# When GpSimd starts, where a decay power is made, one weight difference half a pair later, one split on ScalarE

## The chip, the cores and the metric

The kernel runs on one core of a Trainium2 chip. The metric is the device time of one execution in microseconds (us). The core has five engines with a queue of instructions each: TensorE (PE) for matrix products, VectorE (DVE), ScalarE (ACT), GpSimd (POOL), and SyncE (SP), whose queue issues nearly all DMAs here. An engine works through its queue in order, so an instruction that waits holds up all that stand behind it.

## The reference

Two blocks are chained. The first is a linear attention with decay: for each batch element and head, a 48 x 48 state is multiplied by the decay w and receives the product of k and v at each of 768 steps. The second is a feed-forward block with the activation SoLU, h times softmax(h), followed by a layer norm and an output product.

```python
# r, k, v: (B 4, H 8, S 768, D 48) float32; w, u: (8, 48)
for t in range(S):
    kt, vt, rt = (k[:, :, t], v[:, :, t], r[:, :, t])
    cur = np.einsum('bhd,bhe->bhde', u[None] * kt, vt)
    y[:, :, t] = np.einsum('bhd,bhde->bhe', rt, state + cur)
    state = w[None, :, :, None] * state + np.einsum('bhd,bhe->bhde', kt, vt)
x = y.transpose(0, 2, 1, 3).reshape(B * S, H * D)   # 3072 x 384
h = x @ w_in                                        # 384 -> 1024, weights float64
sm = softmax(h)
solu = h * sm
ln = (solu - mean(solu)) / sqrt(var(solu) + 1e-06) * g_ln
out = ln @ w_out                                    # 1024 -> 384
```

## The kernel before

The sequence is cut into 24 chunks of 128 tokens (6 stretches of time for each of 4 batch elements; chunk `i` and chunk `i + 4` belong to the same batch element). All of a chunk's 8 heads are done together. Chunks are counted from 0. The order of all instructions is written out by hand: each engine's queue is the order of the calls in the program.

**Decay.** The decays w are loaded to `wq` (L494, by SP), transposed on TensorE (`wd_ps`, L636) and raised to powers by VectorE: `pw[:, 0, j]` is w to the power 2^j, and the table `tab` (L655) holds `back`, the powers from w^127 down to w^0, and `fore`, their inverses. Seven products build it, each twice as long as the one before; the last two have 256 and 512 elements in a row. `turn_table` (L663) transposes a table on TensorE and copies it with ScalarE to `kdec` or `rdec`.

**Attention.** For each chunk `decay_k` (L719) multiplies k by `kdec` on GpSimd and makes `kp`; `decay_r` does it with r and makes `rp`; `weigh` multiplies k, u and r on GpSimd (`rku`), and `sum_own` (L738) adds it up on VectorE to `own`, the weight of a token for itself. r and k are transposed. For chunks up to 8 TensorE does this (`turn_r`, `turn_k`), from chunk 9 on a transposing DMA does: `halve_k` (L1034, ScalarE) and `halve_r` (L1040) split the float32 words into 16-bit halves, `turn` issues the DMA from SP, and `join_rk` (L1052, VectorE) puts the words together again. `halve_r` runs on VectorE for chunks below `ON_ACT` and on ScalarE for the others. Then come the scores, their selection by a mask (`take_scores`), the state (`middle`, `update`) and y, which ScalarE copies to `xT`. From chunk 4 on `update` multiplies the new state by w^128 on GpSimd, which it reads from `wide` (L942).

**Feed-forward.** `ffn_in` makes 1024 hidden values in a PSUM tile of which there is one only (`h_ps`); ScalarE takes the exponentials (L957), VectorE multiplies (L964) and so frees `h_ps`. ScalarE then sums the squares. `halve_ln` and `join_ln` (L1017 through `join`) transpose a chunk's 1024 values through the DMA, to `lnT`, and `ffn_out` multiplies by `w_out_sb`. For chunks 4 and up two chunks are multiplied together with seven block products instead of eight, which need differences of blocks of the output weights. `weight_sums` (L1074) makes these on VectorE; the fourth is read in `both_c` (L1152).

**Weights.** They arrive as 64-bit words in 14 pieces of `raw`. `convert_a` (ScalarE), `convert_b` (VectorE) and `convert_c` (GpSimd, an add of integers) make float32 words of them.

**Phases.** The start (L1192 to L1267) does chunks 0 to 4 and converts six pieces. A loop over chunks 2 to 6 follows, one chunk a round. Then come chunks 7 and 8 (L1343 to L1384), and from L1386 a loop over pairs of chunks, of which the first round handles 9 and 10. In that loop `ffn_in`, `ffn_out` and the attention of three different pairs are interleaved. In its first round (`second_pair`) chunk 12's split is called right before `join_ln` of chunk 3.

The call of the differences stands ahead of the pair loop; `first` is chunk 11 in the first round:

```python
    join_ln(l + 2)
    weight_sums((1, 2, 4))
    sum_own(i + 5)
```

Of the kernel before, what the change touches and what calls it, by code (L numbers as in the profile page):

```python
# [9 lines left out]
F32 = mybir.dt.float32  # L10
U32 = mybir.dt.uint32
ACT = mybir.ActivationFunctionType
ALU = mybir.AluOpType
# [386 lines left out]
def direct_path(  # L400
# [29 lines left out]
    nc = tc.nc  # L430
    B, H, S, D = r.shape
    T = 128
    P = U = 64
# [5 lines left out]
    KF = dff // 128  # L439
    NX = 512  # L440
    LA, LO, FIRST, WHOLE, CHECKED = 2, 5, 9, 4, 15
    SEVEN, EARLY, ON_ACT = 4, 12, 13
    ROOM = {18: 4, 19: 5, 20: 3, 21: 2, 22: 1, 23: 0}
    LOW, HIGH = 0.75, 1.25

# [3 lines left out]
    const = ctx.enter_context(tc.tile_pool(name="const", bufs=1))  # L449
# [35 lines left out]
    wq = const.tile([HP, 2, P], F32, name="wq")  # L485
# [4 lines left out]
    w_out_sb = const.tile([128, KF, dm], F32, name="w_out_sb")  # L490
    decays = const.tile([128, HP], F32, name="decays")

    nc.vector.memset(wq, 1.0)
    nc.sync.dma_start(out=wq[:, :, 0:D], in_=w.rearrange("(a q) d -> a q d", q=2))  # L494
    u_row = u_bc[0:1].rearrange("p h d -> p (h d)")
    nc.scalar.dma_start(out=u_row, in_=u.rearrange("h d -> (h d)").unsqueeze(0))
    for i in range(NLD):
# [42 lines left out]
    def convert_b(j):  # L540
        hi, low = step[j]
        n = low.shape[1]
        ma = wpool.tile([128, n], U32, tag="ma", name="ma", bufs=4)
        part = ma
        if pieces[j][2] is None:
            part = psM.tile([128, n], F32, tag="m", name="part").bitcast(U32)

        nc.vector.tensor_scalar(out=part, in0=hi, scalar1=3, scalar2=0x3FFFFFF8,  # L550
                                op0=ALU.logical_shift_left, op1=ALU.bitwise_and)
        nc.vector.scalar_tensor_tensor(out=ma, in0=hi, scalar=0xC0000000, in1=part,  # L552
                                       op0=ALU.bitwise_and, op1=ALU.bitwise_or)
        step[j] = ma, low

    def convert_c(j):
        dst, _, f = pieces[j]
        ma, low = step[j]

        nc.gpsimd.tensor_tensor(out=dst.bitcast(U32) if f is None else ma, in0=ma, in1=low,  # L560
                                op=ALU.add)
# [70 lines left out]
    back, fore = tab[:, 0], tab[:, 1]  # L632
# [30 lines left out]
    def turn_table(table, out, ps):  # L663
        for a in range(HP):
            nc.tensor.transpose(ps[:, a, :], table[:, a, :], ident)
        nc.scalar.copy(out=out, in_=ps)  # L666
# [52 lines left out]
    def decay_k(i):  # L719
        X = live.setdefault(i, {})  # L720
        X["kp"] = apool.tile([128, H, P], F32, name="kp", bufs=5)
        nc.gpsimd.tensor_mul(X["kp"].rearrange("p h d -> p (h d)"),  # L722
                             kpads[i % NLD].rearrange("p h d -> p (h d)"),
                             kdec.rearrange("p a d -> p (a d)"))
# [8 lines left out]
    def weigh(i, engine):  # L733
        rku = live[i]["rku"] = apool.tile([128, H, D], F32, name="rku")
        engine.tensor_mul(rku, kpads[i % NLD][:, :, 0:D], u_bc)  # L735
        engine.tensor_mul(rku, rku, rpads[i % NLD][:, :, 0:D])  # L736
# [315 lines left out]
    def join_rk(i):  # L1052
        X = factors(i)
        join(X["rk"].rearrange("p e a t -> p (e a) t"), X["turned"])
# [19 lines left out]
    def weight_sums(which):  # L1074
        room = {1: tab.rearrange("p e a t -> p (e a t)")[:, 0 : KH * NH],
                2: lows.bitcast(F32).rearrange("p n x -> p (n x)")[:, 0 : KH * NH],
                4: lows.bitcast(F32).rearrange("p n x -> p (n x)")[:, KH * NH : 2 * KH * NH]}
        for n in room:
            room[n] = room[n].rearrange("p (f x) -> p f x", f=KH)
        room[3] = upper[:, :, right]  # L1080
        for n in which:
            t = sums_w[n] = room[n]
            a, b = {1: lambda: (upper[:, :, right], upper[:, :, left]),
                    2: lambda: (lower[:, :, right], sums_w[1]),
                    3: lambda: (lower[:, :, right], upper[:, :, right]),
                    4: lambda: (lower[:, :, left], sums_w[2])}[n]()
            nc.vector.tensor_tensor(out=t, in0=a, in1=b, op=ALU.subtract)
# [104 lines left out]
    turn_r(0)  # L1192
    turn_k(0)
    turn_table(back, kdec, psM.tile([128, HP, 128], F32, tag="m", name="kd_ps"))
    weigh(0, nc.gpsimd)
    decay_k(0)
    sum_own(0)
# [16 lines left out]
    whole_y(0)  # L1214
    whole_outer(0)
    convert_b(1)
    convert_c(1)
    whole_scores(1)
    update(0)
    take_y(0)  # L1220
    decay_k(2)
    weigh(2, nc.gpsimd)
    turn_r(2)
    take_up(2, 0)
# [40 lines left out]
    decay_k(4)  # L1265
    update(2)
    weigh(4, nc.gpsimd)  # L1267


    wide = const.tile([128, H], F32, name="wide")  # L1270
    for q in range(2):
        nc.vector.tensor_copy(out=wide.rearrange("p (a q) -> p a q", q=2)[P : P + D, :, q],
                              in_=pw[q * P : q * P + D, 0, 7])
    todo = list(range(6, len(pieces)))
    now = []
    for i in range(LA, LA + LO):
# [103 lines left out]
    halve_ln(l + 3)  # L1380
    normalise(l + 4)
    join_ln(l + 2)
    weight_sums((1, 2, 4))
    sum_own(i + 5)  # L1384

    for i in range(LA + LO + 2, N, 2):  # L1386
        j, l = i - LA, i - LA - LO
        seven = l >= SEVEN
        for n in (i + 6, i + 7):
            if n < N:  # L1390
                load(n, "kr")
        for n in (i + 3, i + 4):
            if n < N:
                load(n, "v")
        deviation(j - 2, j)
        first, second = ([n] if n < N else [] for n in (i + 2, i + 3))
        for n in first + second:
            diagonal(n)
        if SEVEN <= l <= EARLY:
            row_sums_34(l, nc.gpsimd)  # L1400
        if l < SEVEN:
            decay(i + 4)
        elif i + 4 < N:
            weigh(i + 4, nc.gpsimd)
        decay(i + 5)
        if SEVEN <= l + 2 and i + 6 < N:
            decay_k(i + 6)
            decay_r(i + 6)
        ffn_in(j)
        attend([i, i + 1])  # L1410
        unit_a(j)
        second_pair = i == LA + LO + 2
        if l == EARLY + 4:
            check_next()
        if l < EARLY + 4:
            halve_ln(l + 2)
        else:
            normalise(l + 3)
        if seven:
            both_a(l)  # L1420
        if l == EARLY + 4:
            halve_ln(l + 3)
        for n in (i, i + 1):
            if n < N:
                place(n)
        if i >= CHECKED and l < EARLY + 4:
            check_next()
        unit_b(j)
        if l == EARLY + 4:
            deviation(j, j + 1)  # L1430
        if l <= EARLY:
            normalise(l + 3)
        take([i, i + 1])
        if second_pair:
            halve_rk(i + 3)
        if l == SEVEN:
            weight_sums((3,))
        if seven:
            take_a(l, "DVE")
        else:  # L1440
            join_ln(l + 1)
        check_least()
        for n in first:
            join_rk(n)
        if i + 4 < N:
            halve_rk(i + 4)
        if l == EARLY + 4:
            check_next()
        if seven:
            take_a(l, "ACT")  # L1450
        else:
            ffn_out(l)
        if l > EARLY:
            turn_next(l + 3 if l < EARLY + 4 else l + 4)
        ffn_in(j + 1)
        if seven:
            both_b(l)
        unit_a(j + 1)
        if seven:
            both_c(l)  # L1460
        if l > EARLY:
            check_least()
        if l <= EARLY:
            halve_ln(l + 3)
        else:
            turn_next(l + 4 if l < EARLY + 4 else l + 5)
        if l > EARLY:
            check_next()
        if seven:
            both_d(l)  # L1470
        if l == EARLY + 4:
            join_ln(l + 2)
            join_ln(l + 3)
        for n in (i, i + 1):
            if n < N:
                update(n)
        for n in second:
            join_rk(n)
        if not seven:
            ffn_out(l + 1)  # L1480
        for n in (i + 4, i + 5):
            if n < N:
                sum_own(n)
        for n in (i, i + 1):
            if n < N:
                merged_y(n)
                take_y(n)
        if l > EARLY:
            check_least()
        elif i >= CHECKED - 2:  # L1490
            check_next()
        unit_b(j + 1)
        if l == EARLY + 4:
            deviation(j + 1, j + 2)
        if l <= EARLY:
            normalise(l + 4)
        halve_rk(i + 5)
        if l < EARLY + 4:
            join_ln(l + 2)
            if l + 2 >= SEVEN:  # L1500
                join_ln(l + 3)
        if l + 2 >= SEVEN:
            row_sums_12(l + 2)
        if l + 2 > EARLY:
            row_sums_34(l + 2, nc.vector)
        check_least()
# [89 lines left out]
```

## Time and profile before

| what | us |
|---|---|
| median of 3 runs | 328.79 (328.23 to 329.21) |
| profiled execution, its own time | 326.92 |
| its span | 325.2 |
| TensorE busy | 311.4 (96%) |
| VectorE busy | 257.2 (79%) |
| ScalarE busy | 242.9 (75%) |
| GpSimd busy | 218.5 (67%) |

The span is cut into stretches by what runs in them. Busy time of each engine, from the profile's windows:

| stretch (us) | TensorE | VectorE | ScalarE | GpSimd | share of the DMA engines |
|---|---|---|---|---|---|
| 0 to 30, start | 26.81 | 24.64 | 19.84 | 23.68 | 0.98 |
| 30 to 66, chunks one by one | 34.70 | 34.90 | 30.66 | 28.36 | 0.94 |
| 66 to 91 | 24.06 | 21.68 | 16.77 | 23.44 | 0.95 |
| 91 to 113 | 19.94 | 19.95 | 15.88 | 21.02 | 0.97 |
| 113 to 160, pairs | 46.92 | 42.53 | 40.40 | 45.33 | 0.95 |
| 160 to 220, pairs | 59.41 | 49.02 | 49.07 | 54.68 | 1.00 |
| 220 to 280, pairs | 59.96 | 39.54 | 49.39 | 17.75 | 0.68 |
| 280 to the end | 39.59 | 24.91 | 20.94 | 4.23 | 0.45 |

Start times in the profile count from the beginning of the span. In a line of the timeline the first number is the start, the second the length, then engine, source line, operation, what it writes and reads, how many instructions are merged (x), and in brackets how long the engine stood idle before it and which instruction released it. The chain of waits follows the last instruction back through what released it; "issue" in it is time in which the engine waited for nothing that the profile shows.

### The profile page before, as it was taken

How to read it: one execution, taken by the hardware profiler on the slowest of the kernel's cores; microseconds unless marked ns; L12 is line 12 of the kernel's file. 1: busy time of each engine (PE TensorE's matmuls, PEld its weight loads, DVE VectorE, ACT ScalarE, POOL GpSimd, SP SyncE). 2: the span in 40 equal slices, each digit the busy share in tenths (PEclk: the TensorE clock that was granted, in tenths of full speed). 3: DMA queues.
4: the chain of work that ended last, by engine and by line, in shares of the span. 5: the costliest groups of instructions: out<-in, count | busy, mean ns of one | idle time of the engine just before them, and what ended most of it. 6: DMA issues, size and time to landing. Idle time of an engine off the chain costs nothing.

```text
span 325.2 us, 9669 instructions
## 1 busy us (share of the span) xinstructions
PE 311.4 (96%) x3915; PEld 217.8 (67%) x3915; DVE 257.2 (79%) x437; ACT 242.9 (75%) x413; POOL 218.5 (67%) x235
## 2 busy tenths in 40 slices
PE   8989999999999799999999999999999999999993
PEld 6866555555556366687678668668668667678993
DVE  8896999998888979988798598897579675284571
ACT  5776888888469488968968969959967958957520
POOL 6799778799999999999999999969034020131000
PEclk9999999999999999999999999999999999999998
DMA  6999999889999997998988999998893382873611
GB/s 148 235 267 199 202 191 206 117 140 156 195 169 169 175 147 122 160 184 153 166 184 180 166 211 217 190 203 114 180 197 68 91 191 77 149 168 75 177 71 60
DMA packets 165780, 52.62 MB, mean 162 GB/s; under 512 B 158302, under 2 KB 161503, under 8 KB 165727
## 3 DMA queue, kind: packets, MB, share of 16 engines
q1 hardware_dynamic: 165724, 51.92, 83.5%
q8 instruction: 32, 0.52, 0.7%
q14 instruction: 22, 0.17, 0.2%
q10 hardware_dynamic: 2, 0.00, 0.0%
HBM read 26.75 MB, written 4.72 MB: 97 GB/s over the span
## 4 chain that ended last, share of the span: by engine, by line
PE 65%; POOL 13%; DVE 12%; issue 5%; ACT 1%; DMA 1%; SPq 1%; POOLq 0%; DVEq 0%
PE o_ps L1107 27%; PE h_ps L952 26%; PE y_ps L876 5%; POOL kp L722 3%; PE at L820 2%; DVE ma L552 2%; POOL rp L729 2%; POOL big L755 2%; POOL rku L735 2%; POOL rku L736 2%; PE o_ps L1062 2%; PE kv_ps L903 1%; DVE solu L964 1%; DVE big L833 1%; DVE ma L550 1%
## 5 line engine op out<-in xcount | busy, mean ns | idle before, releaser
L952 PE MATMUL h_ps<-w_in_sb,xT 128*128 128x512 f32 x288 | 129.0, 597 | 0.0
L952 PEld LDWEIGHTS h_ps<-w_in_sb,xT 128*128 128x128 f32 x288 | 53.3, 190 | 59.6 <-issue 57.0
L1023 ACT COPY halves<-solu 128x2048 uint16<-128x2048 uint16 x24 | 45.5, 1896 | 0.2
L984 POOL TENSOR_SCALAR stats<-stats 128x2 f32<-128x2 f32 (+2 forms) x12 | 5.1, 422 | 50.2 <-ACT e L972 49.7
L722 POOL TENSOR_TENSOR kp<-kpad,kdec 128x512 f32<-128x512 f32 x24 | 33.6, 1403 | 4.1 <-ACT kdec L666 2.4
L957 ACT ACTIVATE e<-h_ps 128x1024 f32<-128x1024 f32 x24 | 24.5, 1020 | 12.5 <-PE h_ps L952 12.3
L1017 DVE COPY lnT<-halves 128x2048 uint16<-128x2048 uint16 x18 | 29.8, 1666 | 5.0 <-DMA halves<-halves 5.0
L1017 DVE COPY big<-halves 128x2048 uint16<-128x2048 uint16 x21 | 33.2, 1588 | 0.3
L964 DVE SCALAR_TENSOR_TENSOR solu<-h_ps,stats,e 128x1024 f32<-128x1024 f32 x24 | 30.8, 1284 | 2.2
L755 POOL TENSOR_SCALAR_AFFINE_SELECT big<-own 64x512 f32<-64x512 f32 x40 | 30.1, 752 | 1.7
L736 POOL TENSOR_TENSOR rku<-rku,rpad 128x384 f32<-128x384 f32 x24 | 29.1, 1212 | 1.9
L833 DVE COPY_PREDICATED big<-later_half,at 64x512 f32<-64x512 uint32 x40 | 29.5, 737 | 0.7
L735 POOL TENSOR_TENSOR rku<-kpad,u_bc 128x384 f32<-128x384 f32 x24 | 28.8, 1199 | 1.6 <-ACT u_bc L639 1.6
L962 DVE RECIPROCAL stats<-sums 128x1 f32<-128x1 f32 x24 | 3.8, 159 | 32.4 <-ACT e L957 32.2
L1107 PE MATMUL o_ps<-w_out_sb,ma 128*128 128x192 f32 x160 | 28.4, 329 | 0.1
L998 ACT ACTIVATE solu<-solu,stats 128x1024 f32<-128x1024 f32 x20 | 24.7, 1236 | 4.2 <-POOL stats L992 4.2
L942 POOL TENSOR_TENSOR vt<-vt,wide 48x384 f32<-48x384 f32 x16 | 20.2, 1277 | 10.8 <-DVE vt L939 10.2
L1107 PEld LDWEIGHTS o_ps<-w_out_sb,ma 128*128 128x128 f32 x160 | 26.0, 190 | 1.1 <-issue 0.4
L729 POOL TENSOR_TENSOR rp<-rpad,rdec 128x512 f32<-128x512 f32 x15 | 24.5, 1634 | 0.0
L972 ACT ACTIVATE e<-solu,stats 128x1024 f32<-128x1024 f32 x20 | 22.9, 1146 | 1.4 <-DVE solu L964 1.1
L1062 PE MATMUL o_ps<-w_out_sb,lnT 128*128 128x384 f32 x64 | 21.6, 491 | 2.1 <-DVE lnT L1017 2.1
L876 PE MATMUL y_ps<-big,vt 128*32 128x64 f32 (+1 forms) x1280 | 20.7, 220 | 0.6 <-issue 0.6
(148 smaller groups left out, 611.0 us busy)
## 6 DMA issues: line engine op xcount, KB each, us to landing
raw<-in_moe_w_out_dram SPq DMA_DIRECT2D x16, 384.0 KB, 3.8
kpad<-in_k_dram SPq DMA_DIRECT2D x24, 192.0 KB, 5.2
rpad<-in_r_dram SPq DMA_DIRECT2D x24, 192.0 KB, 5.4
vt<-in_v_dram SPq DMA_DIRECT2D x40, 96.0 KB, 3.8
out_dram<-o SPq DMA_DIRECT2D x20, 192.0 KB, 3.2
raw<-in_moe_w_in_dram SPq DMA_DIRECT2D x7, 512.0 KB, 6.5
raw<-in_moe_w_in_dram SPq DMA_DIRECT2D x10, 256.0 KB, 3.2
vt<-in_v_dram SPq DMA_DIRECT2D x4, 192.0 KB, 6.7
```

The source lines that it names most:

```text
L722: nc.gpsimd.tensor_mul(X["kp"].rearrange("p h d -> p (h d)"), kpads[i % NLD].rearrange("p h d -> p (h d)"), kdec.rearrange("p a d -> p (a ...
L729: nc.gpsimd.tensor_mul(X["rp"].rearrange("p h d -> p (h d)"), rpads[i % NLD].rearrange("p h d -> p (h d)"), rdec.rearrange("p a d -> p (a ...
L735: engine.tensor_mul(rku, kpads[i % NLD][:, :, 0:D], u_bc)
L736: engine.tensor_mul(rku, rku, rpads[i % NLD][:, :, 0:D])
L755: nc.gpsimd.affine_select(out=G[rows, c].rearrange("p a q u -> p (a q) u"), in_=X["own"][rows].to_broadcast([U, H, U]), compare_op=ALU.is_ ...
L833: nc.vector.copy_predicated(X["G"][rows, c].rearrange("p a q u -> p q a u"), later_half[rows].unsqueeze(1).to_broadcast([U, 2, HP, U]), X[ ...
L876: nc.tensor.matmul(y_ps[ts(g, 32), j, ts(c, U)], vf[:, at : at + 32], X["G"][rows, c, h // 2, h % 2, :], start=(g not in opened), stop=las ...
L952: nc.tensor.matmul(h_ps[:, ts(n, NX)], X["xT"][:, j, :], w_in_sb[:, j, ts(n, NX)], start=(j == 0), stop=(j == KD - 1))
L964: nc.vector.scalar_tensor_tensor(out=solu, in0=X["h"], scalar=rs, in1=X["e"], op0=ALU.mult, op1=ALU.mult, accum_out=tot)
L1017: nc.vector.tensor_copy(out=words.bitcast(U16).rearrange("p n (t o) -> p o n t", o=2), in_=turned)
L1023: nc.scalar.copy(out=both.rearrange("p (o n) -> p o n", o=2), in_=split(X["solu"]))
L1107: nc.tensor.matmul(dst, rows[:, f], weights[:, f], start=(start and f == 0), stop=(f == KH - 1), skip_group_check=True)
```

## The change

There are five edits, all of them to the order of work or the engine that does it; what is computed stays the same.

1. The load of w is called ahead of the memset of `wq`, which now covers only the columns that the load doesn't write.
2. `wide`, the power w^128 by head, is made by GpSimd, as the product of w^127 (`back[:, :, 0]`) and w (`pw[:, 0, 0]`), in two instructions right after the call that turns the table, ahead of GpSimd's first `weigh`. Before, VectorE copied it from `pw` later on. So GpSimd's queue, from `weigh(0)` on, stands behind the last product of the table.
3. `decay_k(2)` is called before `convert_c(1)`, no longer after `take_y(0)`. Both are on GpSimd.
4. The fourth difference of output weights (the third to be made) is called in the first round of the pair loop, behind `join_rk` of chunk 11, no longer ahead of that loop.
5. `ON_ACT` is 12 instead of 13: the r split of the chunk with index 12, the thirteenth, is done by ScalarE.

```diff
@@ -439,7 +439,7 @@
-    SEVEN, EARLY, ON_ACT = 4, 12, 13
+    SEVEN, EARLY, ON_ACT = 4, 12, 12
@@ -490,8 +490,8 @@
-    nc.vector.memset(wq, 1.0)
     nc.sync.dma_start(out=wq[:, :, 0:D], in_=w.rearrange("(a q) d -> a q d", q=2))
+    nc.vector.memset(wq[:, :, D:], 1.0)
@@ -1192,6 +1192,14 @@
     turn_table(back, kdec, psM.tile([128, HP, 128], F32, tag="m", name="kd_ps"))
+    wide = const.tile([128, H], F32, name="wide")
+    for q in range(2):
+        rows = slice(q * P, q * P + D)
+        nc.gpsimd.tensor_tensor(out=wide.rearrange("p (a q) -> p a q", q=2)[P : P + D, :, q],
+                                in0=back[rows, :, 0], in1=pw[rows, 0, 0], op=ALU.mult)
     weigh(0, nc.gpsimd)
@@ -1214,11 +1222,11 @@
     convert_b(1)
+    decay_k(2)
     convert_c(1)
     whole_scores(1)
     update(0)
     take_y(0)
-    decay_k(2)
@@ -1265,12 +1273,6 @@
-    wide = const.tile([128, H], F32, name="wide")
-    for q in range(2):
-        nc.vector.tensor_copy(out=wide.rearrange("p (a q) -> p a q", q=2)[P : P + D, :, q],
-                              in_=pw[q * P : q * P + D, 0, 7])
@@ -1380,7 +1382,7 @@
-    weight_sums((1, 2, 4))
+    weight_sums((1, 2))
@@ -1442,6 +1444,8 @@
         for n in first:
             join_rk(n)
+        if second_pair:
+            weight_sums((4,))
         if i + 4 < N:
```

## The prediction

> **What bounds the kernel now.** I read the page first: its busy slices, and the chain of work that ended last by engine. TensorE (PE) carries most of the chain, GpSimd (POOL) and VectorE (DVE) the rest, and GpSimd is full from about a fifth of the span to two thirds.
>
> ```profile
> PE   8989999999999799999999999999999999999993
> DVE  8896999998888979988798598897579675284571
> POOL 6799778799999999999999999969034020131000
> PE 65%; POOL 13%; DVE 12%; issue 5%; ACT 1%; DMA 1%; SPq 1%; POOLq 0%; DVEq 0%
> ```
>
> Shares are averages, so next comes the chain in order of time (start, length, what). Up to 19 us it runs through GpSimd, then TensorE, from 29.67 through VectorE, from 66.68 through GpSimd, and from 113.08 to 280 it is TensorE almost alone.
>
> ```profile
> 5.51 0.69 POOL rku L735
> 6.59 1.06 POOL rku L736
> 7.65 2.39 issue
> 10.07 0.61 POOL kp L722
> ...
> 16.77 1.15 issue
> 17.92 1.29 POOL kp L722
> 19.26 0.66 PE tk_ps L787 x4
> ```
>
> There are two holes here: 2.4 us in which GpSimd waits for `kdec`, and one at 16.8. The timeline of the first 9 us shows why `kdec` is late. The last two table products, of 256 and 512 elements, take 2.58 us from 5.62, beside GpSimd's two products for `rku`:
>
> ```profile
> 5.51 1.01 POOL L735 TENSOR_TENSOR rku<-kpad,u_bc 128x384 f32<-128x384 f32 x1 [1.60 <-ACT u_bc L639]
> 5.62 2.58 DVE L655 TENSOR_TENSOR tab<-tab,pw 128x256 f32<-128x256 f32 x2
> 6.59 1.06 POOL L736 TENSOR_TENSOR rku<-rku,rpad 128x384 f32<-128x384 f32 x1
> ```
>
> The third view is the timeline at 96 to 119 us. It shows what stands before TensorE's only long gap of the steady part (2.14 us; between 113 and 280 the next is 0.6):
>
> ```profile
> 100.25 1.65 DVE L1087 TENSOR_TENSOR lows<-w_out_sb,lows 128x768 f32<-128x768 f32 x1
> 101.16 1.60 POOL L736 TENSOR_TENSOR rku<-rku,rpad 128x384 f32<-128x384 f32 x1
> 102.80 0.55 DVE L740 TENSOR_REDUCE own<-rku 128x8 f32<-128x384 f32 x1 [0.90 <-POOL rku L736]
> 107.73 1.46 DVE L924 TENSOR_TENSOR vt<-kv_ps,vt 48x192 f32<-48x192 f32 x4
> 109.22 1.51 DVE L1044 COPY halves<-rp 128x1024 uint16<-128x1024 uint16 x1
> 110.66 2.37 DVE L1017 COPY lnT<-halves 128x2048 uint16<-128x2048 uint16 x1
> 113.10 1.05 ACT L1038 COPY halves<-kp 128x1024 uint16<-128x1024 uint16 x1 [4.78 <-issue]
> 116.61 0.17 DVE L962 RECIPROCAL stats<-sums 128x1 f32<-128x1 f32 x1 [1.57 <-ACT e L957]
> ```
>
> TensorE is done with the hidden layer of chunk 8 at 110.94. It needs the `lnT` of line 1017, which VectorE ends at 113.03, behind the r split of chunk index 12 and, earlier, the third weight difference.
>
> [...] L736 on GpSimd takes 1.00 us alone and 1.60 at 101.16, beside the difference. [...] The trace has 0.69 for 128x512 at 173.45 (L1097), so the pair in the table needs about 1.1 us, not 2.58.
>
> **The change part by part.** (Own time: the profiled execution is 326.92 us, span 325.2 and 1.7 around it. The median of the runs is 328.79, so 1.87 is added at the end.)
>
> *1. GpSimd behind the table; `wide` on GpSimd; the w load ahead of its memset.* The table ends at about 5.62 + 1.05 = 6.7 instead of 8.2. Not all of this arrives: the transposes to `kd_ps` stand in TensorE's queue behind those of r and k of chunk 0, and their weight load could start at 7.83, not 8.26: 0.43 earlier, and `kdec` with them (9.0 to 9.6). GpSimd begins at 6.7 with two new products of 48x4. No row has that shape; L992, 128x2, costs 0.19 and follows its forerunner by 0.26, so I take 0.5 for both (0.4 to 0.8). Then `rku` 7.2 to 9.3, and `kp` of chunk 0 at 9.6 instead of 10.07. Behind the new wait stand `rku`, `kp`, and for them `own`, the diagonals on ScalarE: `own` would start at 9.4, before it was 9.52. Gain 0.4. The w load leaves SP's queue about 0.25 us sooner (the memset is at 0.87, the issue at 1.06) and with it all loads behind. The table itself starts behind the two PSUM memsets that end at 3.69, so it gains nothing there. The memset of the other columns could wait for that load if the overlap were judged by outline; but the vt memset (L623, at 1.44) comes after the load of vt in the program and ran before it was issued (4.83), so I exclude it.
>
> *2. `kp` of chunk 2 before the add of weight piece 1.* That add waits 0.82 us for VectorE (16.70); a 1.28 product now fills the hole. `kp` ends at 16.8 instead of 19.2, so TensorE's transposes start at 17.4 to 17.8 instead of 19.26. Then `whole_y(1)` waits for the scores' selection on VectorE (17.95 to 19.29, 0.4 earlier by part 1) and starts at about 19.0, not 19.84. The add of piece 1 itself ends where it did, pieces 2 to 5 come up to 1 us sooner. But pieces 4 and 5 hang on their DMA: ScalarE waited 0.77 for the last at 23.09. The hidden layer of chunk 0 therefore ends 0.3 to 0.9 earlier. Parts 1 and 2 together are worth 0.6 at 29.67, where VectorE takes over the chain (bounds 0 and 1.0).
>
> *3. No copies for `wide` on VectorE.* Two copies, 33.00 to 33.34, stand in the chain; VectorE is without idle from 29.67 to 75. Gain 0.35. TensorE has 0.5 to 0.65 of idle in each round there, so it follows. Between 74.6 and 110.94 TensorE has no gap, so this 0.95 arrives at 110.94 whole.
>
> *4. The third difference later.* 1.65 leave VectorE at 100.25. Line 740 waits for GpSimd's L736, which shrinks from 1.60 to 1.00: `own` is 0.6 earlier. It comes back after the join of chunk 11's r and k, where VectorE waited 1.57 for line 957 on ScalarE[...]. Line 957 stood behind line 1038, which began at 113.10 when the `lnT` join had ended (113.03), so it moves too; if the cover were gone, the solu product of line 964 would come at 118.4 instead of 116.88 and still be ahead of TensorE's next use of its bank (120.37). Its readers are in `both_c`, from 140.59.
>
> *5. The r split of chunk 12 on ScalarE.* 1.51 leave VectorE; 1.04 (the eleven others on ScalarE: 1.040 to 1.052) fall into its hole of 4.78. The transpose by DMA is issued some 1.4 sooner.
>
> Parts 4 and 5 take 0.6 + 1.5 = 2.1 from the end of the `lnT` join, which is 113.03 against 110.94 needed: the 2.14 gap goes down to 0.0 or 0.1. Gain 2.1 (1.0 if GpSimd blocks the earlier join for one product more).
>
> *What is late next.* From 113 GpSimd has no idle up to 190. It comes out about 1.3 earlier (0.95 + 0.6, less some of the difference's block), TensorE 3.05. Line 740 at 121.47 had `rku` 1.1 before it was due, and VectorE's line 964 at 128.76 to 130.05 is 1.5 ahead of TensorE at 131.53: together 2.6 of slack, and GpSimd loses 1.8 of it. So it holds; 0.05 is taken for small waits.
>
> Sum: 0.6 + 0.35 + 2.1 - 0.05 = 3.0. Own time 323.9, in terms of the median 325.8 us.
>
> **The rivals.**
> *A. GpSimd becomes the bound after 113.* For it: it is busy 23.2 of 24 us at 113 to 137. Against it: it waits for nobody's sake there, and a pair of chunks takes it 23.2 against TensorE's 23.5. If its lag is 0.8 more than I hold, TensorE loses that in each of two pairs: gain 3.0 - 1.6 = 1.4, time 327.4.
> *B. The start gains nothing, because the weights' DMA sets it.* For it: the DMA engines are 98% busy up to 30 us. Against: only one wait for such a load shows, 0.77. Then 0.35 + 2.1 = 2.45 remain, 326.3.
> *C. Slower: new phases between VectorE and GpSimd [...].* Place: GpSimd's stretch from 66.68 to 102.80, which leads to line 740 and so to the `lnT` join. A blocked product costs about 1.0 (L722 2.21 against 1.28, L736 1.98 against 1.00). About half of its products there are already long. With three more than before the gain is gone, with four it is 1.0 slower: 329.8. Against it: VectorE and GpSimd move by about the same there, since GpSimd waits for VectorE up to 66.68.
>
> **How the numbers follow.** Forecast 0.56, A 0.18, B 0.13, C 0.13. The forecast's own range, from the bounds of parts 1, 2, 4 and 5, is a gain of 4.0 (parts 1 and 2 at 1.0, and 0.6 if GpSimd's blocked products ease as well) down to 1.6 (the earlier join blocked by one product more, with part of the start lost), so 324.8 to 327.2. Range given: 324.4 to 328.3, which takes in A and B; C and a little of both tails are left out. About 0.3% (1.0 us) is what a measurement of this kernel can tell from no change. Faster by more: forecast, B and most of A, 0.77. Within: the rest of A and of C, 0.10. Slower: 0.13.
>
> **What would show it.** L655's pair near 1.1 us and `kp` of chunk 0 near 9.6; `tk_ps` of chunk 2 before 18; line 780, now at 29.67, at about 29.1; no gap of TensorE before the 16 matmuls of 113.08, which begin near 110; the last difference between the joins at 111 to 114 us; no new wait of TensorE up to 165. I am wrong if `kpad` of chunk 2 has not landed when GpSimd comes to it (a DMA wait at 15.5, with piece 1 stuck behind it), if line 740 waits over 2 us at about 119, or if the join of line 1017 still ends after TensorE is free.

## The result, and the profile after

The changed kernel takes 325.9 us in the median (324.62 to 326.83, 15 runs); the kernel before took 327.81 us (326.42 to 329.73, 15 runs, the three of the table above among them). The ratio is 0.9938, with a 95% interval of 0.9917 to 0.9959: faster by 2.0 us (1.3 to 2.7). A second measurement, beside the experiments, gave 0.9954 (0.9934 to 0.9974). The profiled execution is 325.9 us, span 324.2, which is 1.0 us less than the profiled execution of before.

The page of the kernel after, its slices and the chain of waits by engine:

```profile
PE   8999999999999999899999999999999999999993
DVE  7796999998887979988798587988579675284571
POOL 5989778799999999999999999969134020131000
...
PE 53%; DVE 16%; POOL 14%; issue 6%; DMA 4%; ACT 4%; SPq 1%; POOLq 0%; DVEq 0%
```

The slice of TensorE that was at 7 (the fourteenth, at 106 to 114 us) is a 9 now, and the seventeenth, at 130 to 138, has become an 8. TensorE carries less of the chain, 53% where it was 65%, and VectorE, GpSimd, ScalarE and the DMA more. So one gap went and another came further on. The timeline says what they are. First the start:

```profile
5.53 1.11 DVE L655 TENSOR_TENSOR tab<-tab,pw 128x256 f32<-128x256 f32 x2
6.80 0.45 POOL L1201 TENSOR_TENSOR wide<-tab,pw 48x4 f32<-48x4 f32 x2 [2.90 <-DVE tab L655]
9.38 2.51 POOL L722 TENSOR_TENSOR kp<-kpad,kdec 128x512 f32<-128x512 f32 x2
```

The last two products of the table take 1.11 us instead of 2.58, now that GpSimd stands still beside them; the two small products for `wide` cost 0.45; `kp` of chunk 0 begins at 9.38, was 10.07. Then the stretch ahead of the old gap and behind it, on the timeline:

```profile
101.80 0.55 DVE L740 TENSOR_REDUCE own<-rku 128x8 f32<-128x384 f32 x1 [1.98 <-POOL rku L736]
...
107.85 1.04 ACT L1044 COPY halves<-rp 128x1024 uint16<-128x1024 uint16 x1
...
108.22 2.15 DVE L1017 COPY lnT<-halves 128x2048 uint16<-128x2048 uint16 x1
...
110.42 5.43 PE L1062 MATMUL o_ps<-w_out_sb,lnT 128*128 128x384 f32 x16
...
112.56 1.75 DVE L1087 TENSOR_TENSOR lows<-w_out_sb,lows 128x768 f32<-128x768 f32 x1
...
114.48 1.28 DVE L964 SCALAR_TENSOR_TENSOR solu<-h_ps,stats,e 128x1024 f32<-128x1024 f32 x1
```

The sixteen matmuls of line 1062 have no bracket any more: TensorE does not wait, and they begin 2.66 us sooner. The r split is on ScalarE, and the difference of line 1087 lies behind the joins. Up to here all is as it was meant. But what follows is not: the 128 y matmuls at the end of the loop's next round (line 876) begin at 141.30, before at 141.98. Of 2.66 us, 0.68 are left.

Where the rest went is seen on GpSimd and VectorE between 117 and 136. The same instructions, of the kernel before, from its timeline:

```profile
118.29 1.01 POOL L735 TENSOR_TENSOR rku<-kpad,u_bc 128x384 f32<-128x384 f32 x1
119.38 1.01 POOL L736 TENSOR_TENSOR rku<-rku,rpad 128x384 f32<-128x384 f32 x1
...
121.47 0.99 DVE L740 TENSOR_REDUCE own<-rku 128x8 f32<-128x384 f32 x2
122.39 3.75 DVE L1017 COPY lnT<-halves 128x2048 uint16<-128x2048 uint16 x2
...
136.17 0.36 DVE L1133 TENSOR_TENSOR o<-o_ps,o 128x192 f32<-128x192 f32 x1
...
136.68 1.47 PE L1107 MATMUL o_ps<-tab,ma 128*128 128x192 f32 x8
...
141.98 2.00 PE L876 MATMUL y_ps<-big,vt 112*32 112x64 f32 x128
```

and of the kernel after:

```profile
117.32 1.54 DVE L1017 COPY big<-halves 128x2048 uint16<-128x2048 uint16 x1
117.59 2.09 POOL L735 TENSOR_TENSOR rku<-kpad,u_bc 128x384 f32<-128x384 f32 x1
119.76 1.00 POOL L736 TENSOR_TENSOR rku<-rku,rpad 128x384 f32<-128x384 f32 x1
120.80 0.55 DVE L740 TENSOR_REDUCE own<-rku 128x8 f32<-128x384 f32 x1 [1.52 <-POOL rku L736]
121.27 4.20 DVE L1017 COPY lnT<-halves 128x2048 uint16<-128x2048 uint16 x2
...
128.06 1.54 PE L1107 MATMUL o_ps<-lows,ma 128*128 128x192 f32 x8 [0.32 <-DVE stats L962]
...
133.77 1.69 DVE L1087 TENSOR_TENSOR w_out_sb<-w_out_sb 128x768 f32<-128x768 f32 x1
135.49 0.36 DVE L1133 TENSOR_TENSOR o<-o_ps,o 128x192 f32<-128x192 f32 x1
135.90 1.57 PE L1107 MATMUL o_ps<-tab,ma 128*128 128x192 f32 x8 [1.05 <-DVE o L1133]
...
141.30 2.00 PE L876 MATMUL y_ps<-big,vt 112*32 112x64 f32 x128
```

Read it from top to bottom. VectorE's join (line 1017, into `big`) comes when GpSimd is about to multiply k and u of chunk 14 (line 735), and this product takes 2.09 us, not 1.01. So `rku` is ready at 120.76, 0.37 later than before (120.39), though GpSimd was 1.0 ahead at 108. VectorE is there 1.52 too early and waits. It leaves line 740 1.1 sooner than before, and 0.45 of this is lost in the two joins of `lnT` (4.20, before 3.75). From then on it is without a break, through the row sums, line 964, the selections and the third difference (line 1087 at 133.77), up to line 1133, which takes the block out of PSUM that TensorE's next block overwrites. Before, line 1133 ended at 136.53, 0.15 ahead of TensorE. Now TensorE comes 2 us sooner and VectorE 0.68. TensorE feels this in two places: at 128.06, where the block needs the second row sum (line 1098, which ends at 127.91; the profile names the instruction behind it), it falls back by 0.5 us, and at 135.90 by 1.3 more.

### The profile page after: what moved, and what is told of

Its sections match the earlier page's. It is cut to its first block, busy times and chain, and to the rows that moved or that the text cites. A ratio compares the mean times of both kernels' runs of the same rounds, so it can differ in the third digit from the quotient of the medians.

```text
span 324.2 us, 9670 instructions
## 1 busy us (share of the span) xinstructions
PE 311.9 (96%) x3915; PEld 217.4 (67%) x3915; DVE 255.2 (79%) x434; ACT 244.1 (75%) x414; POOL 220.1 (68%) x237
## 4 chain that ended last, share of the span: by engine, by line
PE 53%; DVE 16%; POOL 14%; issue 6%; DMA 4%; ACT 4%; SPq 1%; POOLq 0%; DVEq 0%
PE o_ps L1107 24%; PE h_ps L952 20%; PE y_ps L876 4%; DMA rpad<-in_r_dram 4%; POOL rp L729 3%; POOL big L755 3%; POOL kp L722 3%; POOL rku L735 3%; DVE ma L552 2%; DVE big L833 2%; PE at L820 2%; DVE solu L964 2%; DVE ma L550 1%; PE kv_ps L903 1%; POOL rku L736 1%
## 5 line engine op out<-in xcount | busy, mean ns | idle before, releaser
L984 POOL TENSOR_SCALAR stats<-stats 128x2 f32<-128x2 f32 (+2 forms) x12 | 6.2, 520 | 49.8 <-ACT e L972 49.3
L722 POOL TENSOR_TENSOR kp<-kpad,kdec 128x512 f32<-128x512 f32 x24 | 32.6, 1360 | 1.9 <-DMA kpad<-in_k_dram 1.3
L729 POOL TENSOR_TENSOR rp<-rpad,rdec 128x512 f32<-128x512 f32 x15 | 25.2, 1678 | 0.0
L1062 PE MATMUL o_ps<-w_out_sb,lnT 128*128 128x384 f32 x64 | 21.6, 491 | 0.0
```

The source lines that it names most:

```text
L729: nc.gpsimd.tensor_mul(X["rp"].rearrange("p h d -> p (h d)"), rpads[i % NLD].rearrange("p h d -> p (h d)"), rdec.rearrange("p a d -> p (a ...
```

## The experiments

Theory T: what the gap at 113 gave is given back because GpSimd is late with `rku` of chunk 14; VectorE waits for it at line 740, and line 1133 hands the wait on to TensorE. Rival R: TensorE or GpSimd has no room further on in any case, so that nothing on VectorE would bring it back. Rival S: edits 4 and 5 are each worth their own time up to the end. For the start, the prediction's rival B stands against its steps 1 and 2: the weights' DMA sets it.

Three names in the expectations below need a word. Their "sixteen matmuls of ffn_in(9)" are those of line 1062, which multiply `lnT` of chunk 3. Where they speak of the r split of chunk 13, it is that of the chunk with index 12. And the "third difference", above and below, is `weight_sums((3,))` at 134 us, not the one that edit 4 moves, which is called the fourth.

The table has all kernels. The ratio, with its 95% interval, is of the times of many runs to those of the kernel before in the same job; the rest is from one profile each: start of the first line 780; of the matmuls of line 1062 and TensorE's wait ahead of them; VectorE's wait for `rku` of chunk 14; start of the y matmuls near 141; how long the stretch from line 1062 to these took (us).

| kernel | ratio | L780 | L1062 (wait) | wait L740 | y | stretch |
|---|---|---|---|---|---|---|
| before | | 29.67 | 113.08 (2.14) | 0 | 141.98 | 28.90 |
| after | 0.9938 (0.9917 to 0.9959) | 29.20 | 110.42 (0) | 1.52 | 141.30 | 30.88 |
| after_again | 0.9954 (0.9934 to 0.9974) | 30.27 | 110.55 (0) | 1.52 | 141.42 | 30.87 |
| start_only | 0.9966 (0.9944 to 0.9989) | 30.06 | 113.40 (2.13) | 0 | 142.32 | 28.92 |
| stall_only | 0.9965 (0.9945 to 0.9985) | 30.69 | 111.72 (0) | 1.52 | 142.61 | 30.89 |
| w3_late | 0.9917 (0.9888 to 0.9947) | 30.43 | 110.72 (0) | 1.52 | 141.07 | 30.35 |
| own_late | 0.9905 (0.9873 to 0.9937) | 30.31 | 110.98 (0) | 0 | 140.65 | 29.67 |
| own_w3_late | 0.9908 (0.9881 to 0.9936) | 29.22 | 110.39 (0) | 0 | 139.79 | 29.40 |
| no_w4 | 0.9955 (0.9938 to 0.9972) | 29.13 | 110.41 (0.46) | 0.43 | 140.58 | 30.17 |
| no_act | 0.9966 (0.9948 to 0.9983) | 29.41 | 111.77 (1.52) | 0.45 | 141.32 | 29.55 |
| own_stall | 0.9937 (0.9916 to 0.9959) | 29.76 | 110.95 (0) | 0 | 140.64 | 29.69 |
| own_only | 1.0008 (0.9988 to 1.0027) | 30.66 | 113.85 (2.10) | 0 | 142.78 | 28.93 |
| kp2_only | 1.0004 (0.9979 to 1.0029) | 29.62 | 112.83 (2.12) | 0 | 141.77 | 28.94 |
| gate_wide_only | 0.9987 (0.9969 to 1.0005) | 29.46 | 112.36 (2.12) | 0 | 142.94 | 30.58 |

**The change in two halves.** `start_only` is the kernel before with edits 1 to 3, which is the changed kernel with edits 4 and 5 undone as below; `stall_only` is the kernel before with these same lines the other way round:

```diff
-    SEVEN, EARLY, ON_ACT = 4, 12, 12
+    SEVEN, EARLY, ON_ACT = 4, 12, 13
...
-    weight_sums((1, 2))
+    weight_sums((1, 2, 4))
...
-        if second_pair:
-            weight_sums((4,))
```

> Edits 1 to 3 alone (w load, wide on GpSimd behind the table, kp of chunk 2 earlier); ON_ACT 13 and the fourth difference ahead of the loop, as before. Theory T (the start brings what the trace of the changed kernel shows at 110, 0.4 us): 0.4 us faster than before, TensorE's gap ahead of the 16 matmuls of line 1062 at 113 still 2.0 to 2.2 us. Rival (the start brings the forecast's 0.95): 0.9 to 1.0 us faster.

> Edits 4 and 5 alone (fourth difference in the loop, r split of chunk 12 on ScalarE), start as before. Theory T (edits 4 and 5 take the whole gap at 113, and VectorE gives most of it back ahead of line 1133): gap at 113 below 0.2 us, a new gap of TensorE of 0.7 to 1.5 us at line 1107 some 23 us later, total 0.5 to 1.7 us faster than before. Rival (nothing is given back without the start's edits): 2.1 us faster.

Measured: 0.9966 and 0.9965. Each half is worth about 1.1 us (0.4 to 1.8), and the two together 2.0 or 1.5; within these intervals the halves may add up or not. For `start_only` this is nearer to the rival's 0.9 to 1.0 than to the 0.4 that T had from one trace, and its own trace shows no gain at all at line 1062 (113.40, before 113.08); see the part on the start. With `stall_only` the gap of 2.1 us is gone, but the stretch up to y grows by 1.99 us, the same as with the whole change, and the wait of 1.52 us is there. With `start_only` the gap stays and the stretch is that of before. So the give-back in this stretch belongs to edits 4 and 5, not to the start's edits.

**Loosening the chain at two places.** `own_late` is the whole change, with the row sum of chunk 14 (and no other) called behind the row sums of the stage; `w3_late` has the third difference behind line 1133 instead of ahead of it:

```diff
-            if n < N:
+            if n < N and not (second_pair and n == i + 5):
                 sum_own(n)
...
             row_sums_34(l + 2, nc.vector)
+        if second_pair:
+            sum_own(i + 5)
```

```diff
-        if l == SEVEN:
-            weight_sums((3,))
         if seven:
             take_a(l, "DVE")
         else:
             join_ln(l + 1)
+        if l == SEVEN:
+            weight_sums((3,))
```

> The changed kernel, with line 740 of chunk 14 called behind the row sums of the pair instead of ahead of both lnT joins, so that VectorE doesn't stand waiting for GpSimd's rku (1.52 us). Theory T (GpSimd's lag starts the new gap): VectorE is 0.8 to 1.5 us earlier at line 1133, TensorE's gap there falls to 0.0 to 0.3, total 0.8 to 1.3 us faster than the changed kernel. Rival (the transposing DMA of lnT, [...] keeps the joins where they are): VectorE waits at line 1017 instead, within 0.3 us of the changed kernel.

> The changed kernel, with the third difference called behind line 1133's add instead of ahead of it. Theory T (TensorE's new gap at 135.9 is line 1133 standing behind VectorE's string, whose last piece is this difference, 1.69 us): the gap goes, 0.8 to 1.1 us faster than the changed kernel. Rival (the block product with that difference then waits as long): within 0.3 us of it.

`own_late` took 0.9905, and the stretch shrank from 30.88 to 29.67. Its timeline:

```profile
119.28 0.53 DVE L740 TENSOR_REDUCE own<-rku 128x8 f32<-128x384 f32 x1
119.73 1.67 DVE L1017 COPY lnT<-halves 128x2048 uint16<-128x2048 uint16 x1
122.48 2.18 DVE L1017 COPY lnT<-halves 128x2048 uint16<-128x2048 uint16 x1 [1.08 <-DMA halves<-halves]
...
133.85 0.96 DVE L1087 TENSOR_TENSOR w_out_sb<-w_out_sb 128x768 f32<-128x768 f32 x1
134.84 0.36 DVE L1133 TENSOR_TENSOR o<-o_ps,o 128x192 f32<-128x192 f32 x1
135.25 1.57 PE L1107 MATMUL o_ps<-tab,ma 128*128 128x192 f32 x8 [0.30 <-DVE o L1133]
```

The wait for `rku` is gone, the first join, which stood behind it in VectorE's queue, is 1.54 us sooner (119.73, was 121.27), and what VectorE waits for next is the transposing DMA (1.08). So, counted from line 1062, VectorE is only 0.48 earlier at the third difference; 0.73 more come because this now takes 0.96 us instead of 1.69. In the kernel after this difference ran beside GpSimd's products of lines 1103 (from 133.38) and 735 (from 134.60); what made it shorter in `own_late` isn't shown. TensorE's wait for line 1133 is 0.30, was 1.05. `w3_late` leaves the wait of 1.52 where it is and takes only the last link; its stretch is 0.53 shorter, less than the 0.8 to 1.1 expected, because TensorE then waits 0.52 at the next addition in VectorE's queue, line 1151. Both places lie on the chain that T names. R would have kept 30.9.

**Both, and each of edits 4 and 5 undone.** These four ran on one chip: the change once more (`after_again`), `own_w3_late` with both loosenings, `no_w4` with the fourth difference back ahead of the loop (edit 4 undone), `no_act` with `ON_ACT` at 13 (edit 5 undone). In the diff of `start_only` above, the first pair of lines is the edit of `no_act` and the rest that of `no_w4`; `own_w3_late` has both diffs of the loosenings.

> The kernel with the whole change, unaltered, as the yardstick of the next three on one chip. From its own runs (ratio 0.994 to the kernel before): 0.992 to 0.996; the waits of VectorE for rku of chunk 14 (about 1.5 us at 120.8) and of TensorE for its o block (about 1.0 us at 136) should stand again, within 0.3 us each.

> The whole change, and both loosenings: the row sum of chunk 14 behind the stage's row sums, and the third difference of output weights one addition later. Theory T (the gain of the gap at 113 is given back because VectorE waits for GpSimd's rku of chunk 14, and the third difference then delays the read of o): from the first of the sixteen matmuls of ffn_in(9) to the last y matmul 29.2 to 29.7 us (30.9 with the whole change alone, 29.7 with the first loosening), no gap above 0.3 us before the o block at 136; 1.0 to 1.6 us faster than the whole change. Rival R (the give-back is one of TensorE's own queue, and whatever is loosened on VectorE returns further on): 30.4 to 31, no faster than the whole change.

> The whole change with the fourth difference back ahead of the loop. Theory T: VectorE comes about 1.7 us later to the join at 108, so TensorE has a gap of 0.3 to 1.2 us again ahead of ffn_in(9), but VectorE is at chunk 14's row sum when GpSimd is, so the wait of 1.5 us there falls to below 0.3 and the total is within 0.5 us of the whole change, on either side. Rival S (parts 4 and 5 are each worth their own time to the end): 1.0 us or more slower than the whole change.

> The whole change with the r split of chunk 13 back on VectorE. Theory T: VectorE is 0.9 to 1.2 us later at the join, a gap of 0.2 to 1.0 us ahead of ffn_in(9), and a wait for rku of chunk 14 that is smaller by as much; total within 0.5 us of the whole change. Rival S: 0.9 us or more slower than the whole change.

`own_w3_late` is the fastest by its profile: stretch 29.40, span 322.0, median 324.14 us (six runs) beside 325.87 for the change; by its ratio, 0.9908, it can't be told from `own_late`, and the intervals of it and of the change (0.9881 to 0.9936, 0.9934 to 0.9974) barely touch. Beside `w3_late`, from which only the moved row sum sets it apart, VectorE comes to line 1133 1.26 sooner, counted from line 1062, and the stretch is 0.95 shorter: this is the most direct measure of what the wait for `rku` cost. The 0.50 by which the stretch is still longer than before falls at line 1151, for which TensorE waits 0.24. The other two are a test of T from the other side. Their lines at the head of the stretch, first `no_w4`:

```profile
110.41 5.43 PE L1062 MATMUL o_ps<-w_out_sb,lnT 128*128 128x384 f32 x16 [0.46 <-DVE lnT L1017]
...
117.00 1.00 POOL L735 TENSOR_TENSOR rku<-kpad,u_bc 128x384 f32<-128x384 f32 x1
117.16 2.04 DVE L1017 COPY big<-halves 128x2048 uint16<-128x2048 uint16 x1
...
120.05 0.55 DVE L740 TENSOR_REDUCE own<-rku 128x8 f32<-128x384 f32 x1 [0.43 <-POOL rku L736]
```

then `no_act`:

```profile
111.77 5.43 PE L1062 MATMUL o_ps<-w_out_sb,lnT 128*128 128x384 f32 x16 [1.52 <-DVE lnT L1017]
...
120.80 0.55 DVE L740 TENSOR_REDUCE own<-rku 128x8 f32<-128x384 f32 x1 [0.45 <-POOL rku L736]
```

With edit 4 undone TensorE has 0.46 us of the gap again, with edit 5 undone 1.52: so the prediction's prices for the two edits, 0.6 and 1.5, were right at that place (the expectation for `no_act`, 0.2 to 1.0, was too low). But the time hardly moves: 0.9955 and 0.9966 beside 0.9954, in the medians 0.31 and 0.44 us slower, where S asked for 1.0 and 0.9. In `no_act` y begins at 141.32, as with the whole change, though TensorE stood still 1.5 us longer at 110: the wait at line 740 is 1.07 smaller, and VectorE leaves it at the same moment, 120.80. So S doesn't hold. In `no_w4` VectorE still waits 0.43, a little more than T allowed, but line 735 keeps its short length there (1.00 us), so that VectorE begins line 740 0.75 sooner, and y begins 0.72 sooner than with the change. A longer pause of TensorE at 214 (1.15 us for 0.36, see the end) then takes all of it. So in these profiles edit 4, added to the others, gained nothing by 141 and may have cost something.

**The loosening without the start, and alone.** `own_stall` is `stall_only` with the row sum moved as in the diff of `own_late`, `own_only` the kernel before with nothing but that.

> The two edits at the gap of 113 (fourth difference, r split) without those of the start, and the row sum of chunk 14 behind the stage's row sums. Theory T (the gap's gain was lost at that row sum): no wait of VectorE for rku of chunk 14; from the first of the sixteen matmuls of ffn_in(9) to the last y matmul of 141 to 143 29.4 to 29.9 us (30.9 with the two edits alone), that y matmul 1.0 to 1.3 us earlier than with the two edits alone, and the whole 0.4 to 0.7% faster than before. Rival R (what is gained at 113 is lost on TensorE or GpSimd further on in any case): 30.5 us or more, 0.3% or less.

> The kernel before with only that row sum moved. Theory T: with TensorE's gap of 2.1 us still in place VectorE never waited there, so nothing is gained: within 0.3% of before, the y matmul near 142 within 0.3 us of 28.9 after ffn_in(9) begins. Rival O (the row sum's place is worth something by itself): 0.4% or more faster.

Measured: 0.9937 for the first (0.9965 without the move, in another job) and 1.0008 for the second. The move is worth nothing where the gap at 113 stands. Where it is gone it is worth 0.9 us by the ratios, which come from two jobs and have intervals of 0.7 either way, and 1.2 in the stretch. (That y begins 1.97 sooner than in `stall_only`, and not 1.0 to 1.3, is in part the start: line 780 is 0.93 sooner there.) That is the mark of a wait that was hidden behind another one.

**The start, part by part.** `kp2_only` is the kernel before with edit 3 alone; `gate_wide_only` has edits 1 and 2 and leaves edit 3 out.

```diff
     convert_b(1)
+    decay_k(2)
     convert_c(1)
     whole_scores(1)
     update(0)
     take_y(0)
-    decay_k(2)
```

> The kernel before with only decay_k(2) ahead of convert_c(1). If the hole of GpSimd at 16.8 is worth time (step 2 of the prediction): tk_ps of chunk 2 at 17.8 to 18.3 instead of 19.26, the hidden layer of chunk 0 beginning 0.5 to 1.0 us sooner, line 780 at 29.2 to 29.6 (29.67 before). Rival B (the weights' DMA sets the start): ScalarE waits for raw longer by what TensorE gains, the hidden layer of chunk 0 ends within 0.2 us of 27.6, no gain.

> The kernel before with edits 1 and 2 of the list (w load first, wide on GpSimd behind the table) and decay_k(2) left where it was. Step 1: kp of chunk 0 at 9.4 to 9.7 (10.07), kp of chunk 2 at 17.5 (17.92), line 780 0.2 to 0.5 us sooner, and the next line 780 0.5 to 0.8 sooner because the copies for wide are gone. Rival B: the first line 780 within 0.2 us of 29.67, ScalarE's wait for the third raw above 1 us.

Edit 3 alone did what it says, and it brought nothing. TensorE and ScalarE in `kp2_only`, from its timeline:

```profile
17.40 0.60 PE L787 MATMUL tk_ps<-ident,kp 128*128 128x128 f32 x4
...
20.09 0.69 ACT L537 ACTIVATE lows<-raw 128x512 uint32<-128x512 uint32 x1 [1.22 <-DMA raw<-in_moe_w_in_dram]
...
21.46 4.87 PE L952 MATMUL h_ps<-w_in_sb,xT 128*128 128x512 f32 x10
26.52 1.12 PE L952 MATMUL h_ps<-w_in_sb,xT 128*128 128x512 f32 x2 [0.19 <-POOL w_in_sb L560]
```

The transposes come at 17.40 (19.26 before), the hidden layer of chunk 0 begins at 21.46 (22.21), and it ends at 27.64 (27.69), since its last piece of weights is not there sooner. ScalarE's wait for the piece at 20 us has grown from nothing to 1.22. The first line 780 gains 0.05, and the ratio is 1.0004. That is rival B's mechanism, for this one edit. `gate_wide_only` gains 0.21 at line 780 and, by its ratio, 0.4 us or nothing; the stretch in its profile is not to be used, since TensorE ran at a lower clock there (see below). The parts' ratios don't add up to that of `start_only`, but their intervals allow it.

The eight profiled kernels with all three edits of the start have line 780 at 29.13 to 30.43, 29.75 in the mean; the four with none of them have it at 29.67 to 30.69, 30.20 in the mean. The spread follows a DMA: the piece of `raw` that ScalarE turns to at about 20 us lands so that this begins anywhere from 19.60 to 20.89 in the former. The gain of 0.45 is therefore no more than a difference of two means whose single values lie up to 1.3 us apart, and it isn't shown safely.

What the missing copies for `wide` gave, 0.37, is steadier at first: from the first line 780 to the second it is 3.71 us with them (4.7 in the two profiles that began latest), and 3.33 to 3.34 without. Then it can be lost. In the kernel after, GpSimd's `kp` of chunk 5 waits for its DMA and begins at 33.90, and then:

```profile
35.14 1.19 POOL L735 TENSOR_TENSOR rku<-kpad,u_bc 128x384 f32<-128x384 f32 x1
...
36.67 1.15 DVE L550 TENSOR_SCALAR ma<-raw 128x384 uint32<-128x384 uint32 x1
...
39.02 0.68 DVE L780 TENSOR_TENSOR big<-tr_ps,tab 128x512 f32<-128x512 f32 x1
```

Line 550 takes 0.35 us in `no_w4`, where `kp` of chunk 5 began at 33.13, and 1.15 here, beside GpSimd's line 736. So the third line 780 comes 6.48 us after the second in the kernel after, 5.95 in `no_w4`. Three of the eight profiles with these edits show the long form. And an early start is not worth its whole length further on: the same kernel, profiled twice (after, `after_again`), has the first line 780 at 29.20 and 30.27, the third at 39.02 and 39.19, and line 1062 at 110.42 and 110.55. What the three edits of the start are worth stays open for this reason: 0.39 at 110 in the one pair of profiles before and after, but 1.1 (0.4 to 1.8) by the times of `start_only`.

**The granted clock behind the gap.** The granted clock is, in the profile's view, TensorE's share of full speed. In the profile of `gate_wide_only`, which has the gap of TensorE still, it is lower right behind the gap, and 1.00 from 105 to 112 us and from 118 to 124. First the line of the timeline, then the view of the window from 112 to 118 us, in which 0.72 is the mean granted clock:

```profile
112.36 7.12 PE L1062 MATMUL o_ps<-w_out_sb,lnT 128*128 128x384 f32 x16 [2.12 <-DVE lnT L1017]
...
112.00:118.00 6.00, 5.64 (x12) 3.20 (x13) 4.28 (x7) 5.26 (x6) 5.92 (x5) 0.72 0.78 151
```

The sixteen matmuls take 1.69 us more than the 5.43 of every other profile (at a mean clock of 0.72, 0.28 of the window's 6.00 us are missing, 1.68), and the mean clock of this execution is 0.991, that of the other profiled ones 0.996 or more. The record has this mean for every run of the experiments. Below 0.996 are 69 of 164 runs of the kernel before and 31 of 79 of the four other kernels that keep the gap of 2.1 us. Of the kernels with a gap of 1.52 us or none it is 6 of 139, among them 1 of the 37 of the kernel after, its first measurement included. The runs below are slower: in the three jobs of the experiments the kernel before has medians of 328.5 to 328.9 us below 0.996 and of 326.8 to 327.6 from there up.

So a part of what edits 4 and 5 gave seems to be that this loss has become rare. Among runs with a clock of 0.996 or more the medians leave 1.0 us of the 1.5 that `after_again` gained, 1.0 for `start_only` and 0.4 for `stall_only`. The limit of 0.996 was chosen after the fact, and only one trace shows where in the run the clock falls, so this is a reading of the record and not an experiment.

## Why the prediction was right, and where it was wrong

The forecast, 325.8 us, stands beside 325.9, but this is better than the reasoning deserves. It took 3.0 us off a median of three runs (328.79), and in all later measurements the kernel before had a median 0.7 to 1.4 lower (327.4 to 328.06). So the agreement is luck: a gain that was forecast too large was taken from a time that was too long. The gain is 2.0 in one measurement and 1.5 in the other. Direction and most mechanisms held; of the gain that was forecast, a half to two thirds came, and about 0.5 of that seems to be the clock, of which the prediction has nothing.

- *Step 1, the table.* Right in the numbers that it named as signs: pair of products 1.1 (1.11), `wide` 0.5 (0.45), `kp` of chunk 0 at 9.6 (9.38 to 9.86 in the profiles). The 1.1 was the author's estimate: of the pair's two lengths the trace of before has the longer, 0.69 for 128x512 at 173.45, and for 128x128 it has 0.27, at 5.29, which puts 128x256 near 0.4. Measured, the pair took 2.58 us beside GpSimd's products (1.80 in `kp2_only`), 1.11 without them.
- *Step 2, `kp` of chunk 2.* The order worked, `tk_ps` at 17.41. The gain didn't follow: 0.05 at line 780 with this edit alone. The prediction itself had noted that the pieces hang on their DMA, and yet counted part of it. Together with step 1: 0.47 at line 780 in the profile, 0.45 in the mean, where 0.6 was said.
- *Step 3, the copies.* 0.37 leave VectorE, where 0.35 was said. But "it follows" was too sure: in the profiled execution 0.46 went to a collision with GpSimd's products for chunk 5, which had hardly moved (`kp` at 33.90, before 34.12), because their DMA hadn't landed. At 110 all the start's edits were worth 0.39 there, not 0.95. The times of `start_only` (1.1, from 0.4 to 1.8) don't exclude the 0.95, so whether this sum was wrong stays open.
- *Steps 4 and 5.* The difference of edit 4 (the prediction calls it the third, as it is the third to be made) and the r split cost the `lnT` join what was said, 0.6 and 1.5: the gap went down to 0, and putting them back gave 0.46 and 1.52. Such a difference took 0.96 us in `own_late` at 133.85; the four of the kernel before, each beside products of GpSimd, took 1.65 to 2.02.
- *What is late next: the step that failed.* It has two terms, and both were mis-sized. GpSimd was to come out about 1.3 us earlier at `rku` of chunk 14; it came 0.37 later. It was ahead by 1.0 at 108, and then `rp` at 109.15 took 2.32 (before 1.71) and line 735 at 117.59 took 2.09 (before 1.01), each beside a join of VectorE that now came at another moment; line 736 between them gave back 0.33. And the slack behind it was taken as 1.1 at line 740 and 1.5 at line 964, 2.6 together. For chunk 14, the second of the two row sums at 121.47, the first was about 1.5. But what VectorE then hands on is limited by the tightest reader of its queue, and this was not line 964 but line 1133, further on, which was 0.15 ahead of TensorE. With it even the forecast's lag of 1.8 was too much for the slack that it had counted (1.1 + 0.15). The lag was 3.0 (2.66 and 0.37); less 1.5 and 0.15 this leaves 1.4, and 0.45 came in the two joins of `lnT`. So not 0.05 was lost, but 1.98 between line 1062 and y. TensorE's two new waits, 0.32 and 1.05, speak against the prediction's sign of no new wait up to 165. `own_late` brought back 1.2 of the 1.98, `own_w3_late` 1.5.
- *The rivals.* A had the mechanism, GpSimd's lag behind 113, and its gain of 1.4 is nearer to the 1.5 and 2.0 measured than the forecast's 3.0. But it put the loss as 0.8 in each of two pairs; it was one round of the loop, and 2.0. B is true of edit 3, but not of the start as a whole by the times of `start_only`. C's new collisions came, at 36 and at 109 to 119 rather than at 66 to 103, and they didn't turn the sign.

## What to carry to other kernels

When a stall is taken away, follow every engine that had slack because of it through the next two rounds, and write down how far ahead of its reader each result was. A lag is taken up once at each hand-over from one engine to the next, and within the queue of one engine it is the smallest slack of all its readers that counts (here the 0.15 us of line 1133, not the 1.5 of line 964 ahead of it). Try edits that shorten the same wait apart: either of two could be left out here at 0.3 to 0.4 us. Try again what was worth nothing while the stall stood, since a row sum called later was worth about 1 us only when it was gone. And look at the granted clock of all runs, not only of the profiled one: a gain can lie in a loss that has become rare.

## What the runs showed of the hardware

- GpSimd's products of the same shape have a short length and longer ones. Between 100 and 125 us line 735 is 0.99 to 1.02 or 2.02 to 2.09, line 736 1.00 to 1.02, 1.60 or 1.93 to 1.96, `rp` 1.27 to 1.31, 1.71 to 1.72 or 2.32 to 2.35. In the kernel after the long ones ran beside VectorE's joins (line 1017) or the difference of line 1087; line 736 at 119.76, with nothing of VectorE beside it, took 1.00. In the chunk-14 place the long line 735 appeared in the seven profiles in which the gap at 113 was wholly gone, and the short one in the seven others. In the former VectorE's join begins 0.27 to 0.31 us ahead of line 735, in the latter at least 0.16 behind it (`no_w4`: 117.16 and 117.00). So a shift of two engines by some tenths goes with it; no run moved the join alone.
- Behind a wait of TensorE of 2.12 us the granted clock was 0.72 in the mean of 6 us in one profile (`gate_wide_only`, 112 to 118), and a mean clock below 0.996 is found in 100 of 243 runs of the kernels with a wait of 2.1 us there, and in none of the 22 runs of `no_act`, with a wait of 1.52.
- TensorE has one pause, marked "issue", in the middle of the y matmuls at 212 to 217 us, of 0.36 to 1.20 us in the kernels before and after and in nine others (0.59 before, 0.36 after, 1.15 in `no_w4`). In `own_late`, `own_w3_late` and `own_stall` it isn't there, and from y at 141 to the last y, at 282 to 286, these take 142.55 to 142.59 us, the kernel before 143.41. So a part of what these three gain in time is this pause. `own_only` has the moved row sum too, and has the pause (0.71). What makes it wasn't tried and stays open.
